# Last two row blocks of w_out in loads over seven, seven and fifteen DMA engines

## Chip, cores and metric

The kernel runs on one core of one Trainium2 chip. The metric is the device time of one execution in microseconds. The kernel before takes 129.38 us (median of three runs, 129.35 to 129.42). The profile comes from one further execution, which took 129.8 us by itself.

## What is computed

One token, a row x of 576 numbers, is normalised (xn) and goes through two branches whose results are added to x.

```python
# A: attention over the last W = 4096 cached keys, 32 query heads, 16 key/value heads, Dh = 128
q = xn @ wq                                   # (576 x 4096)
p = softmax(q . k[-4096:] * Dh**-0.5)
a = (p . v[-4096:]) @ wo                      # (4096 x 576)
# B: gated MLP, F = 4608, Fh = 2304, one position
z = gelu(xn @ w_in)                           # (576 x 4608)
g = w_sp * layernorm(z[Fh:]) + b_sp           # w_sp, b_sp are scalars here
b = (z[:Fh] * g) @ w_out                      # (2304 x 576)
out = x + a + b
```

All inputs are bf16. The caches are 65536 positions long, of which 4096 are read. With the weights that makes 50.96 MB read from HBM, and hardly any arithmetic per byte.

## The kernel before

All large loads are issued by SP, in one order written out by hand (`tc.manual_schedule`): wq (two loads of two 8 KB rows per partition each, L129 and L130), the rest of wq (`wq_h`, L131), w_in (L132 to L134), then the key and value pairs (`load_k`, `load_v` through `load_pair`, L100 to L112), and last, from step u = 13 of the main loop on (L443 to L455), w_out and wo. A pair is a tile of 128 partitions x 16 KB. It comes in one load of 2 MB, or in two halves of 8 KB per partition: the key pairs 0 and 1, and the value pair 7. Six buffers hold pairs, so a load of a pair waits until TensorE is through with the pair six before it.

Every load signals its landing on one of eight semaphores, which are taken in turn. A load therefore also waits until the load eight places before it has landed. In the trace a landing is a row of sixteen increments of the semaphore, one for each DMA engine that carried a share.

TensorE transposes the keys (L338), forms the scores (L355), transposes the probabilities (L372) and multiplies them with the values (L402). At the end it projects: `project` (L457) does two matmuls, one for each half of the 576 outputs: a single column of 128 numbers times 128 x 288 weights, summed into `sps_130` and `sps_131`. I call the two a pair of matmuls. There is a pair for each of 32 columns of the attention output (`wo_sb`) and each of the 18 row blocks of w_out (`wout_sb`).

The row blocks of w_out are grouped by `WOUT_CHUNKS` (L39). An entry (i, t0, t1) is the rows t0 to t1 of each group of nine rows, in half i of w_out; partition p holds rows 9p to 9p+8 of that half. So (0, 0, 9) is one load of 10368 bytes per partition, and (1, 0, 5), (1, 5, 8), (1, 8, 9) are loads of 5760, 3456 and 1152 bytes per partition. In the profile they are `wout_0_310`, `wout_0_311`, `wout_5_312` and `wout_8_313`. The order of the last loads is: value pair 7 in two halves, `wout_0_310`, the five loads of wo, `wout_0_311`, `wout_5_312`, `wout_8_313`. TensorE uses them at the end in the same order, but for `wout_0_310`, which is used before wo (L472, L486). After the last pair of matmuls VectorE and ScalarE each cast one half of the row (L501, L502), and SP stores it (L503).

Of the kernel before, what the change touches and what calls it, by code (L numbers as in the profile page):

```python
# [16 lines left out]
D = 576  # L17
# [14 lines left out]
ZC = 1152  # L32
# [3 lines left out]
NZ1 = 18  # L36
KV_BUFS = 6
WO_CHUNKS = ((0, 0, 8), (1, 0, 8), (2, 0, 8), (3, 0, 4), (3, 4, 8))
WOUT_CHUNKS = ((0, 0, 9), (1, 0, 5), (1, 5, 8), (1, 8, 9))  # L39


@with_exitstack
def kernel(
# [14 lines left out]
    nc = tc.nc  # L58
    P = nc.NUM_PARTITIONS
# [22 lines left out]
    def wrows(src, t0, t1):  # L82
        return src[0:512, :].rearrange("(p t) c -> p t c", t=4)[:, t0:t1, :]

    def whalf(src):
        return src[512:576, :].rearrange("m (c j) -> (m c) j", c=2)

    wq_t = wpool.tile([P, 4, 4096], BF16, name="wq")
# [8 lines left out]
    def pair_rows(cache, jp):  # L97
        return cache[0, 2 * jp:2 * jp + 2, SK - W:SK, :].rearrange("h (k t) d -> k h (t d)", k=64)

    def load_pair(cache, jp, nm, halves):  # L100
        tile_ = kvpool.tile([P, 64, DH], BF16, name=f"{nm}{jp}", tag="kv")
        dst, src = tile_[:].rearrange("p t d -> p (t d)"), pair_rows(cache, jp)
        n = 8192 // halves
        for f in range(halves):
            nc.sync.dma_start(dst[:, n * f:n * (f + 1)], src[:, :, n * f:n * (f + 1)])
        return tile_

    def load_k(jp):
        kn_tiles[jp] = load_pair(A_k_cache, jp, "kn", 2 if jp < 2 else 1)

    def load_v(jp):
        v_tiles[jp] = load_pair(A_v_cache, jp, "v", 2 if jp == 7 else 1)  # L112
# [13 lines left out]
    order = tc.manual_schedule(engines={PE, SP})  # L126
    ctx.enter_context(order)

    for t in range(2):  # L129
        nc.sync.dma_start(wq_t[:, 2 * t:2 * t + 2, :], wrows(A_wq, 2 * t, 2 * t + 2))  # L130
    nc.sync.dma_start(wq_h[:], whalf(A_wq))  # L131
    for t in range(4):  # L132
        nc.sync.dma_start(win_sb[t][:], wrows(B_w_in, t, t + 1).rearrange("p t c -> p (t c)"))
# [143 lines left out]
    def z_columns():  # L277
        zv = zrow[:].rearrange("p (c t) -> p t c", t=9)
        for t in range(9):
            nc.tensor.matmul(  # L280
                fin[:, MZ + 4 * t:MZ + 4 * t + 4], lhsT=zv[:, t, :], rhs=id4f[:], start=True, stop=True,
            )
        zsb = const.tile([P, NZ], FP32, name="zsb")
        nc.vector.tensor_copy(
            zsb[:].rearrange("p (i t) -> p i t", i=4),
            fin[:, MZ:MZ + NZ].rearrange("p (t i) -> p i t", i=4),
        )
        u = const.tile([P, NZ], FP32, name="u_gelu")
        nc.vector.tensor_mul(u[:], zsb[:], zsb[:])
        nc.vector.tensor_scalar(out=u[:], in0=u[:], scalar1=0.044715, scalar2=1.0, op0=ALU.mult, op1=ALU.add)  # L290
        nc.vector.tensor_mul(u[:], u[:], zsb[:])
        th = const.tile([P, NZ], FP32, name="th_gelu")
        nc.scalar.activation(th[:], u[:], ACT.Exp, scale=-2.0 * GELU_C)
        nc.vector.tensor_scalar_add(th[:], th[:], 1.0)
        nc.vector.reciprocal(th[:], th[:])
        G = const.tile([P, NZ], FP32, name="G_gelu")
        nc.vector.tensor_mul(G[:], th[:], zsb[:])
        statz = const.tile([P, 2], FP32, name="statz")
        nc.vector.reduce_sum(statz[:, 0:1], G[:, NZ1:NZ], axis=AXX)
        junk2 = work.tile([P, NZ1], FP32, name="junk")  # L300
        nc.vector.tensor_tensor_reduce(
            out=junk2[:], in0=G[:, NZ1:NZ], in1=G[:, NZ1:NZ], scale=1.0, scalar=0.0,
            op0=ALU.mult, op1=ALU.add, accum_out=statz[:, 1:2],
        )
        return G, statz
# [3 lines left out]
    def z_gate(G, statz):  # L309
        mvz = mean_rstd(statz, FH, "z")  # L310
        z2n = const.tile([P, NZ1], FP32, name="z2n")
        nc.vector.tensor_scalar(out=z2n[:], in0=G[:, NZ1:NZ], scalar1=mvz[:, 0:1], scalar2=mvz[:, 3:4],
                                op0=ALU.subtract, op1=ALU.mult)
        gv = const.tile([P, NZ1], FP32, name="gv")
        nc.vector.tensor_scalar(out=gv[:], in0=z2n[:], scalar1=sb_col[:, 0:1], scalar2=sb_col[:, 1:2],
                                op0=ALU.mult, op1=ALU.add)
        nc.vector.tensor_mul(hv[:], G[:, 0:NZ1], gv[:])

    w2pool = tc.alloc_tile_pool(name="w2pool", bufs=1, reuse_waits="tile")
    wo_sb = [w2pool.tile([P, r1 - r0, D], BF16, name=f"wo{g}_{r0}") for g, r0, r1 in WO_CHUNKS]  # L320
    wout_sb = [w2pool.tile([P, t1 - t0, D], BF16, name=f"wout{i}_{t0}") for i, t0, t1 in WOUT_CHUNKS]

# [8 lines left out]
    def transpose_k(u):  # L331
        jp, half = u // 2, u % 2
        kn = kn_tiles[jp]
        parts = []
        for c in range(4):
            tps = ps_t.tile([P, 8, P], BF16, name=f"ktps{u}_{c}", tag="tps")
            for s in range(8):
                nc.tensor.transpose(tps[:, s, :], kn[:, 32 * half + 8 * c + s, :], ident[:])  # L338
            kT = ktpool.tile([P, 1024], BF16, name=f"kT{u}_{c}", tag="kT")
            src = tps[:].rearrange("p a b -> p (a b)")  # L340
            if c % 2:
                nc.scalar.copy(kT[:], src)
            else:
                nc.vector.tensor_copy(kT[:], src)
            parts.append(kT)
        kT_tiles[u] = parts
# [20 lines left out]
    def transpose_p(g):  # L367
        p_sb = p_tiles.pop(g)
        ptps = ps_t.tile([P, 8, P], BF16, name=f"ptps{g}", tag="tps")
        for b in range(2):  # L370
            for s in range(4):
                nc.tensor.transpose(  # L372
                    ptps[:, 4 * b + s, 0:NR], p_sb[0:NR, b, 128 * s:128 * (s + 1)], ident[0:NR, 0:NR])
        ptq = ptq_sb[g % 2]
        for m in range(2):
            for half in range(2):
                r0 = 8 * half + 4 * m
                for b in range(2):
                    for h in range(2):
                        nc.vector.tensor_scalar(  # L380
                            out=ptq[:, m, half, b, :, :].rearrange("p i (k c) -> p k i c", c=4)[
                                :, 4 * m:4 * m + 4, :, 2 * h:2 * h + 2],
                            in0=ptps[:, 4 * b:4 * b + 4, :].rearrange("p s (i r) -> p s i r", i=4)[
                                :, :, :, r0 + 2 * h:r0 + 2 * h + 2],
                            scalar1=BIG, scalar2=mask2[:, h:h + 1], op0=ALU.min, op1=ALU.mult,
                        )
            nc.vector.tensor_reduce(
                out=psum_all[:, 8 * g + 4 * m:8 * g + 4 * m + 4],
                in_=ptq[:, m, :, :, :, 16 * m:16 * m + 16].rearrange("p f b i (s c) -> p c (f b i) s", c=4),
                op=ALU.add, axis=mybir.AxisListType.XY,  # L390
            )
# [30 lines left out]
    for u in range(22):  # L422
        if u < 16:
            transpose_k(u)
        if u == 0:
            gz = z_columns()
        if u == 1:
            z_gate(*gz)
        if u in (5, 9, 13, 17):
            transpose_p((u - 5) // 4)  # L430
        if u == 17:
            den = ps_t.tile([P, 512], FP32, name="den", tag="tps")
            nc.tensor.matmul(den[0:HQ, 0:1], lhsT=psum_all[:], rhs=ones_f[:, 0:1], start=True, stop=True)
            rden = const.tile([HQ, 1], FP32, name="rden")
            nc.vector.reciprocal(rden[:], den[0:HQ, 0:1])
        if u in (10, 14, 18):
            o_rows((u - 10) // 4)
        if 1 <= u <= 16:
            scores(u - 1)
        if u >= 6:  # L440
            pv(u - 6)
        load_next(more.get(u, 0))
        if u == 13:  # L443
            def load_wout(n):
                i, t0, t1 = WOUT_CHUNKS[n]
                nc.sync.dma_start(
                    wout_sb[n][:],
                    B_w_out[ZC * i:ZC * (i + 1), :].rearrange("(p t) n -> p t n", t=9)[:, t0:t1, :])

            load_wout(0)  # L450
            for n, (g, r0, r1) in enumerate(WO_CHUNKS):
                nc.sync.dma_start(
                    wo_sb[n][:], A_wo[1024 * g:1024 * (g + 1), :].rearrange("(p r) n -> p r n", r=8)[:, r0:r1, :])
            for n in range(1, len(WOUT_CHUNKS)):
                load_wout(n)  # L455
# [8 lines left out]
    def project_b(n, ts):  # L464
        i, t0, t1 = WOUT_CHUNKS[n]
        for t in ts:
# [27 lines left out]
    for n, (g, r0, r1) in enumerate(WO_CHUNKS):  # L494
        for r in range(r0, r1):
            project(oT_all[:, r, g:g + 1], wo_sb[n][:, r - r0, :])
    for n in range(1, len(WOUT_CHUNKS)):
        project_b(n, range(WOUT_CHUNKS[n][1], WOUT_CHUNKS[n][2]))

# [35 lines left out]
```

## Time and profile before

| What | Value |
|---|---|
| median of three runs | 129.38 us |
| the profiled execution | 129.8 us, of which its span 127.8 us |
| read from HBM | 50.96 MB, 399 GB/s over the span |
| DMA queue q1 (all of SP's loads) | 95.3% of sixteen engines' span |
| TensorE busy | 69% of the span, granted clock 0.888 on average |
| DVE and ACT busy | 35% and 33% |
| landing of `wout_0_311` | 122.91 us |
| last matmul starts | 124.76 us |
| store of the output issued | 125.82 us |

The span runs from the first to the last instruction. The profiled execution's own time is 2.0 us longer than its span. "PEclk" is the share of TensorE's full clock that was granted. The "DMA" row is the mean busy share of the sixteen DMA engines.

### The profile page before, as it was taken

To read this page: it belongs to the slowest core of one execution; us is meant where nothing else is said; L and a number is where in the kernel's file an instruction comes from. 1 tells how busy PE (TensorE), PEld (TensorE's weight loads), DVE (VectorE), ACT (ScalarE), POOL (GpSimd) and SP (SyncE) were. 2 spreads that over 40 slices of the span, in tenths; PEclk is the share of its full clock that TensorE was granted. 3 is DMA by queue.
4 is the path that set the end of the run, shared out by engine and by line. 5 is a ranking of instruction groups with operands and counts; after the bars stand their busy time and mean duration, and the time that the engine had idled before them with its cause. 6 is when DMAs were issued, how large, how long until landed. Compare 5 with 4: busy or idle time off the path is not lost.

```text
span 127.8 us, 2524 instructions
## 1 busy us (share of the span) xinstructions
PE 88.5 (69%) x1080; PEld 62.7 (49%) x1080; DVE 45.1 (35%) x161; ACT 41.7 (33%) x50; POOL 3.7 (3%) x10
## 2 busy tenths in 40 slices
PE   1014953463999999895399797299399907977761
PEld 0012221123999688662377475287198404545430
DVE  3043110030307756982033944045842290022001
ACT  4000010010503778655056566049243701031001
POOL 8001000000000100000000000000000000000000
PEclk9999999999995999999657999869959995589975
DMA  5999999999999999999999999999999999999950
GB/s 129 436 421 396 437 430 424 410 422 423 413 446 431 446 410 413 441 421 426 410 436 431 431 426 405 451 415 433 405 441 431 392 428 412 419 430 410 412 205 0
DMA packets 5202, 51.11 MB, mean 400 GB/s; under 512 B 582, under 2 KB 712, under 8 KB 1480
## 3 DMA queue, kind: packets, MB, share of 16 engines
q1 hardware_dynamic: 5186, 50.96, 95.3%
q8 instruction: 8, 0.13, 0.4%
q14 instruction: 2, 0.02, 0.0%
q10 hardware_dynamic: 6, 0.00, 0.0%
HBM read 50.96 MB, written 0.00 MB: 399 GB/s over the span
## 4 chain that ended last, share of the span: by engine, by line
DMA 68%; PE 27%; DVE 2%; SPq 1%; issue 0%; DVEq 0%
DMA kn_816<-in_A_k_cache_dram 18%; DMA kn_101<-in_A_k_cache_dram 17%; DMA wout_0_311<-in_B_w_out_dram 15%; DMA v_1254<-in_A_v_cache_dram 12%; DMA wq<-in_A_wq_dram 6%; PE fin L280 3%; DVE ptq_314 L380 2%; PE sps_130 L355 2%; PE sps_130 L459 2%; PE sps_131 L355 1%; PE ops L402 1%; PE ktps_0_1102 L338 1%; PE ktps_0_318 L338 1%; PE ktps_0_387 L338 1%; PE ktps_2_1124 L338 1%; PE ktps_2_409 L338 1%
## 5 line engine op out<-in xcount | busy, mean ns | idle before, releaser
L338 PEld LDWEIGHTS <-kn_101 128*128 128x128 bf16 x64 | 6.6, 148 | 3.5 <-DMA kn_101<-in_A_k_cache_dram 3.5
L338 PEld LDWEIGHTS <-kn_450 128*128 128x128 bf16 x64 | 5.3, 124 | 4.9 <-DMA kn_450<-in_A_k_cache_dram 4.0
L338 PEld LDWEIGHTS <-kn_816 128*128 128x128 bf16 x64 | 5.1, 123 | 4.0 <-DMA kn_816<-in_A_k_cache_dram 3.6
L338 PEld LDWEIGHTS <-kn_972 128*128 128x128 bf16 x64 | 4.9, 118 | 3.0 <-DMA kn_972<-in_A_k_cache_dram 2.6
L265 PEld LDWEIGHTS <-xz 128*32 128x32 bf16 x60 | 2.3, 123 | 8.3 <-issue 7.0
L237 ACT CAST qrow<-sps_131 128x512 bf16<-128x512 f32 x1 | 0.6, 585 | 12.8 <-PE sps_131 L231 12.8
L338 PEld LDWEIGHTS <-kn_692 128*128 128x128 bf16 x64 | 3.6, 98 | 1.9 <-DMA kn_692<-in_A_k_cache_dram 1.4
L338 PEld LDWEIGHTS <-kn_111 128*128 128x128 bf16 x64 | 3.6, 98 | 1.8 <-DMA kn_111<-in_A_k_cache_dram 0.9
L280 PEld LDWEIGHTS fin<-id4f,zrow 128*128 128x128 f32 x18 | 4.4, 336 | 0.0
L280 PE MATMUL fin<-id4f,zrow 128*128 128x4 f32 x18 | 4.4, 377 | 0.0
L272 ACT COPY zrow<-zps_234 128x384 f32<-128x384 f32 x1 | 0.5, 478 | 11.2 <-PE zps_234 L265 11.2
L271 DVE COPY zrow<-zps_233 128x384 f32<-128x384 f32 x1 | 0.6, 558 | 10.1 <-PE zps_233 L265 10.1
L402 PEld LDWEIGHTS <-ptq_315 128*32 128x32 bf16 x64 | 3.2, 118 | 1.8 <-issue 0.3
L459 PEld LDWEIGHTS <-oT_all 128*1 128x1 bf16 x64 | 2.7, 83 | 2.8 <-issue 1.0
L338 PEld LDWEIGHTS <-kn_107 128*128 128x128 bf16 x64 | 3.6, 98 | 0.9 <-issue 0.9
L338 PEld LDWEIGHTS <-kn_104 128*128 128x128 bf16 x64 | 3.6, 98 | 0.9 <-issue 0.9
L166 PE MATMUL fin<-sb_row,one_row 1*128 1x2 bf16 x1 | 0.2, 182 | 5.3 <-DMA sb_row<-in_B_b_sp_dram 5.3
L231 PE MATMUL sps_130<-wq,xz 128*32 128x512 bf16 x16 | 2.5, 628 | 1.6 <-DVE xz L198 1.6
L502 ACT CAST res<-sps_131 1x288 bf16<-1x288 f32 x1 | 0.4, 389 | 9.8 <-PE sps_131 L459 9.8
L338 PE MATMUL ktps_0_818<-ident,kn_450 128*128 128x128 bf16 x8 | 1.0, 308 | 3.5 <-DMA kn_450<-in_A_k_cache_dram 3.5
L501 DVE CAST res<-sps_130 1x288 bf16<-1x288 f32 x1 | 0.4, 446 | 8.6 <-PE sps_131 L459 8.6
L380 DVE TENSOR_SCALAR ptq_315<-ptps_1409,mask_128 128x32 bf16<-128x32 bf16 x16 | 2.5, 236 | 2.5 <-PE ptps_1409 L372 2.5
(352 smaller groups left out, 233.9 us busy)
## 6 DMA issues: line engine op xcount, KB each, us to landing
wq<-in_A_wq_dram SPq DMA_DIRECT2D x2, 2048.0 KB, 9.5
kn_101<-in_A_k_cache_dram SPq DMA_DIRECT2D x2, 1024.0 KB, 20.2
kn_104<-in_A_k_cache_dram SPq DMA_DIRECT2D x2, 1024.0 KB, 21.3
kn_107<-in_A_k_cache_dram SPq DMA_DIRECT2D x1, 2048.0 KB
v_109<-in_A_v_cache_dram SPq DMA_DIRECT2D x1, 2048.0 KB
kn_111<-in_A_k_cache_dram SPq DMA_DIRECT2D x1, 2048.0 KB, 27.5
v_113<-in_A_v_cache_dram SPq DMA_DIRECT2D x1, 2048.0 KB
kn_450<-in_A_k_cache_dram SPq DMA_DIRECT2D x1, 2048.0 KB
```

The source lines that it names most:

```text
L231: nc.tensor.matmul(sps[b][32 * i:32 * i + 32, :], lhsT=lhsT, rhs=rhs, start=(t == 0), stop=(t == 4), tile_position=(0, 32 * i),)
L237: nc.scalar.copy(qrow[:, 512:1024], sps[1][:])
L265: nc.tensor.matmul(zps[b][32 * i:32 * i + 32, 0:ZB], lhsT=lhsT, rhs=rhs, start=(t == 0), stop=(t == 4), tile_position=(0, 32 * i),)
L271: nc.vector.tensor_copy(zrow[:, 0:ZB], zps[0][:, 0:ZB])
L272: nc.scalar.copy(zrow[:, ZB:2 * ZB], zps[1][:, 0:ZB])
L280: nc.tensor.matmul(fin[:, MZ + 4 * t:MZ + 4 * t + 4], lhsT=zv[:, t, :], rhs=id4f[:], start=True, stop=True,)
L338: nc.tensor.transpose(tps[:, s, :], kn[:, 32 * half + 8 * c + s, :], ident[:])
L355: nc.tensor.matmul(sps[b][32 * i:32 * i + 16, :], lhsT=q_bf[:, g, m, half, :], rhs=parts[c // 2][:, 512 * (c % 2):512 * (c % 2) + 512], st ...
L380: nc.vector.tensor_scalar(out=ptq[:, m, half, b, :, :].rearrange("p i (k c) -> p k i c", c=4)[:, 4 * m:4 * m + 4, :, 2 * h:2 * h + 2], in0 ...
L402: nc.tensor.matmul(ops[32 * i:32 * i + 32, :], lhsT=ptq[:, m, half, b, i, :], rhs=v[:, t0:t0 + 4, :], start=(u % 4 == 0 and b == 0), stop= ...
L459: nc.tensor.matmul(outp[g], lhsT=lhsT, rhs=rhs[:, OC * g:OC * (g + 1)], start=first, stop=last, tile_position=(0, 32 * g),)
L501: nc.vector.tensor_copy(res[:, 0:OC], outp[0])
```

## The change

The last three loads of w_out become five pieces in a different cut. Row block (1, 0, 5) stays. Then come row blocks 5 and 6 in one load over sixteen engines (2304 bytes per partition), and row blocks 7 and 8 in three loads by partitions: 0 to 48, 49 to 97 and 98 to 127, again with 2304 bytes per partition. The two pieces of 49 partitions are carried by seven DMA engines, seven partitions each; the piece of 30 by fifteen, two partitions each. All other large loads are of 128 partitions, eight for each of sixteen engines. Two loads elsewhere are merged: the two loads of wq become one of 32 KB per partition, and key pair 1 comes in one load of 2 MB and no longer in two halves. The number of loads that SP issues stays the same.

```diff
-WOUT_CHUNKS = ((0, 0, 9), (1, 0, 5), (1, 5, 8), (1, 8, 9))
+WOUT_CHUNKS = ((0, 0, 9), (1, 0, 5), (1, 5, 7), (1, 7, 9))
+
+TAIL_ROWS = ((0, 49), (49, 98), (98, 128))
...
-        kn_tiles[jp] = load_pair(A_k_cache, jp, "kn", 2 if jp < 2 else 1)
+        kn_tiles[jp] = load_pair(A_k_cache, jp, "kn", 2 if jp < 1 else 1)
...
-    for t in range(2):
-        nc.sync.dma_start(wq_t[:, 2 * t:2 * t + 2, :], wrows(A_wq, 2 * t, 2 * t + 2))
+    nc.sync.dma_start(wq_t[:], wrows(A_wq, 0, 4))
...
-                nc.sync.dma_start(
-                    wout_sb[n][:],
-                    B_w_out[ZC * i:ZC * (i + 1), :].rearrange("(p t) n -> p t n", t=9)[:, t0:t1, :])
+                dst = wout_sb[n][:].rearrange("p t n -> p (t n)")
+                src = B_w_out[ZC * i:ZC * (i + 1), :].rearrange("(p t) n -> p (t n)", t=9)[:, D * t0:D * t1]
+                for p0, p1 in TAIL_ROWS if n == len(WOUT_CHUNKS) - 1 else ((0, P),):
+                    nc.sync.dma_start(dst[p0:p1, :], src[p0:p1, :])
```

## The prediction

> **What bounds the kernel now.** I read the page first, from its slices and its queues.
>
> ```profile
> DMA  5999999999999999999999999999999999999950
> ...
> q1 hardware_dynamic: 5186, 50.96, 95.3%
> q8 instruction: 8, 0.13, 0.4%
> q14 instruction: 2, 0.02, 0.0%
> ```
>
> The DMA engines are full from the second slice to the 38th, so the stream of 50.96 MB sets the time, and only the head, the tail and the overhead of packets can be won or lost. The ten packets of kind "instruction" are fetches of code: eight of 16 KB, two of 8 KB. Next I read the end of the chain of waits.
>
> ```profile
> 104.31 18.61 DMA wout_0_311<-in_B_w_out_dram
> 122.91 0.04 issue
> 122.96 0.33 PE sps_130 L459
> ...
> 125.31 0.45 DVE res L501
> ```
>
> `wout_0_311` lands at 122.91 us, and TensorE then runs nine pairs of matmuls without a pause; the timeline shows where the two later loads come in.
>
> ```profile
> 123.80 0.45 PE L459 MATMUL sps_130<-wout_0_311,hv 128*1 128x288 bf16 x1
> 124.04 0.45 PE L459 MATMUL sps_130<-wout_5_312,hv 128*1 128x288 bf16 x1
> 124.52 0.45 PE L459 MATMUL sps_130<-wout_5_312,hv 128*1 128x288 bf16 x1
> 124.76 0.45 PE L459 MATMUL sps_130<-wout_8_313,hv 128*1 128x288 bf16 x1
> ```
>
> A pair costs 0.24 us here, because the granted clock fell to 0.50 after 123 us; at full clock earlier pairs start 0.12 us apart. The issues say that `wout_5_312` lands at 106.80 + 17.2 = 124.0 us and `wout_8_313` at 109.96 + 14.3 = 124.3 us. So TensorE's slow run of nine pairs only just covers the last landing: 124.76 - 124.30 = 0.46 us are to spare. Last, the windows of the end, whose final two columns are DMA share and GB/s:
>
> ```profile
> 121.50:122.00 0.50, 0.35 (x6) 0.11 (x3) 0.00 (x0) 0.00 (x0) 0.00 (x0) 1.00 1.08 431
> 122.00:122.20 0.20, 0.00 (x0) 0.00 (x0) 0.00 (x0) 0.00 (x0) 0.00 (x0) 1.00 0.70 271
> 122.80:123.00 0.20, 0.04 (x2) 0.04 (x3) 0.00 (x0) 0.00 (x0) 0.00 (x0) 1.00 0.63 248
> 123.40:123.60 0.20, 0.20 (x6) 0.10 (x4) 0.00 (x0) 0.00 (x0) 0.00 (x0) 0.50 0.46 156
> 123.60:123.80 0.20, 0.20 (x5) 0.10 (x2) 0.00 (x0) 0.00 (x0) 0.00 (x0) 0.50 0.40 144
> 123.80:124.00 0.20, 0.20 (x4) 0.13 (x1) 0.00 (x0) 0.00 (x0) 0.00 (x0) 0.50 0.06 17
> ```
>
> The engines don't end together: about six stop by 122.1, the rest run to 123.9. The sixteen increments of each load's semaphore, which the trace records, say it exactly. For `wout_8_313` six come at 122.51 to 122.90, two at 123.60 and 123.69, eight at 124.03 to 124.30. Those groups match the fetches: eight engines carried 16 KB of code each and are some 1.5 us late, two carried 8 KB and are some 0.9 us late, six carried none. (A 16 KB fetch took 1.02 to 1.12 us in the trace, against 0.61 us for a data packet of that size.) A share moved off the late engines is what could be won, at most 0.8 us, the distance from the mean of the sixteen (123.54) to the last.
>
> **The change, part by part.**
>
> *Merged loads.* Key pair 1: eight packets of 16 KB at 613 ns stand for sixteen of 8 KB at 312 ns on every engine; consecutive packets overlap by 4 ns, so 8 x (2 x 308 - 609) = 0.06 us, and one 9 ns marker packet goes. For wq, a row of 32 KB is not in the trace: at one end it is cut into packets of 16 KB as now (only a marker goes, 0.01 us), at the other it saves as key pair 1 does, 0.06 us more. It can't add packets, so no loss. I take 0.08 us in all: every later landing moves up by that.
>
> What waits for the merged wq: the matmuls on its first half start at 11.40 and would start after the second half's landing, 12.93, so 1.5 us later. The q and first z matmuls end then near 19.4 us; the next w_in load releases matmuls at 19.83 after 1.64 us of waiting, which hides it. Without that cover it would still be hidden, since the DMA stream doesn't wait for these matmuls. Key pair 1 is first transposed at 42.3 us and landed whole at 38.1: hidden. Before the first wait for a landing SP can issue the merged wq, wq_h and w_in's four large loads: 9.2 MB, some 21 us of stream at 430 GB/s. So the shifted turns of the eight semaphores starve nothing.
>
> *Issue at the end.* Each piece waits for the load eight places before it: the first piece takes the place that `wout_8_313` has now (109.96), the second waits for the first load of wo (landed 112.73), the third for the second (115.52). SP has nothing queued behind them but the store, at 125.8. Five issues at 0.33 us each are over by 116 us, while the engines are busy with earlier loads until after 120.5: hidden by 4 us.
>
> *Row blocks 5 to 8.* Now an engine carries 8 packets of 3456 and 8 of 1152 bytes after `wout_0_311`, which step by 131 and 47 ns (135 and 51 ns less the overlap): 1.42 us. A packet of 2304 bytes isn't in the trace; halfway between it steps by 89 ns. Eight engines' worth of equal cut would again be 16 x 89 = 1.42 us. After the change, a piece over seven engines gives each 7 packets, the third piece gives two to fifteen. If both pieces of seven use the same engines, these seven carry 8 + 7 + 7 + 2 = 24 packets, 2.14 us (0.72 more), eight others 10, 0.89 us (0.53 less), the last 8, 0.71 us (0.71 less). If the second piece takes another seven, fourteen carry 17 and nothing moves by more than 0.1 us. I take the same seven: the four packets of ACT's second and third small load, which go over one engine, stand at 5.510, 6.123, 6.736 and 7.349 us, exactly one 16 KB packet (613 ns) apart, so they queue on one and the same engine. No row tells their numbers.
>
> *Which engines are late.* Ten of sixteen are late, so of any seven at least one is. Nine engines get less, ten would need it. If the one among the seven is an 8 KB one, its landing goes from 123.69 to 124.41 us; if it is a 16 KB one, from 124.30 to 125.02. Eight engines of sixteen are of the second kind; if they stand in a row (round the circle), 14 of the 16 placements touch a given seven, and scattered nearly all do. So I take 125.02.
>
> *The end.* The last load now feeds two pairs and not one. With 125.02, pair 17 starts at 125.07 and pair 18, at half clock, at 125.31, against 124.76 now: 0.55 us later. Less 0.08 us: +0.47 us. On the profiled execution that is 129.8 + 0.47 = 130.27; the difference applied to the median gives 129.38 + 0.47 = **129.85 us**. (The profiled execution is 0.4 us over the median; its clock at the end may have been lower than in the other runs. At full clock the last pair starts now at 124.35 and then at 125.19: +0.76 us net.)
>
> [...] The rows show every engine at one speed, 16384 bytes in 609 ns, whether sixteen are busy or seven (135 ns for 3456 bytes at 120.6 and at 123.1). By that, moving rows to idle engines moves time. [...]
>
> **Rivals.**
>
> *Hidden.* Only an 8 KB engine is among the seven. The last landing is 124.41 - 0.08 = 124.33 us, still covered by TensorE's nine slow pairs: pair 17 at 124.52 as now. Then only the merged loads count: 129.30 us, no change. It speaks for it that the chain runs through `wout_0_311`, which isn't touched; against it, the count of eight in sixteen.
>
> *Faster.* The runs without a profile end on the last landing, at full clock, and the late engines stand all among the nine that get less (then the 8 KB fetches must cost less there). The last landing is the late ones' 124.30 - 0.53 = 123.77, one pair more costs 0.12, the merged loads give 0.08: -0.49 us, 128.89 us. It decides from the point where the clock stays at 1.0 past 123 us; that three runs agree within 0.07 us speaks for a landing and not for a clock that falls at some moment.
>
> *Collisions.* The pieces slow each other and the late engines. Priced by the nearest row, a packet beside a fetch, which takes 1.09 us for 0.61: half of the 0.72 us extra again, and twice over the two pieces: at full clock 129.38 + 0.76 + 0.7 = 130.8 us as the far end.
>
> **How the numbers follow.** A measurement tells 0.2% (0.26 us) from no change. Forecast 0.42, collisions 0.08: slower 0.5. Hidden 0.3: same. Faster 0.2. The range takes in faster and hidden, and the forecast up to full clock and a little contention: 128.9 to 130.3 us.
>
> **What would show it.** In the profile after, the last piece's increments: seven engines' shares should land late, one at about 125.0, others about 0.5 us earlier than now; a wait of TensorE on the last load ahead of pair 17; no pause of DMA before 122 us; `wout_0_311` near 122.83. It is wrong if the last landing lies before 124.4 us, if the increments of the two pieces come from fourteen engines, or if the clock at the end differs.

## The result, and the profile after

The changed kernel takes 130.95 us (median of four runs, 130.65 to 131.13) against 129.40 us beside it. The ratio, taken over all executions and not between the medians, is 1.0105, with a 95% interval of 1.0064 to 1.0146: slower by some 1.4 us (0.8 to 1.9), where 0.47 us had been forecast. The profiled execution has a span of 129.1 us, 1.3 us more than before.

The page's DMA slices show the same full stream, but the last slices fall off differently (its GB/s row ends with 410 358 85 0, that of before with 410 412 205 0, in slices that are 1% longer).

```profile
DMA  6979999999999999999999999999999999999930
```

The end of the chain of waits now runs through the last load, where it ran through `wout_0_311` (now named `wout_0_309`):

```profile
115.59 10.20 DMA wout_7_311<-in_B_w_out_dram
125.79 0.14 issue
125.92 0.40 PE sps_128 L461
...
126.67 0.45 DVE res L503
```

The last piece lands at 125.79 us; before, the last landing was at 124.30. In the timeline TensorE pauses before each of the three groups of row blocks:

```profile
123.33 0.28 PE L461 MATMUL sps_128<-wout_0_309,hv 128*1 128x288 bf16 x1 [1.42 <-DMA wout_0_309<-in_B_w_out_dram]
...
124.62 0.28 PE L461 MATMUL sps_128<-wout_5_310,hv 128*1 128x288 bf16 x1 [0.52 <-DMA wout_5_310<-in_B_w_out_dram]
...
125.92 0.40 PE L461 MATMUL sps_128<-wout_7_311,hv 128*1 128x288 bf16 x1 [0.77 <-DMA wout_7_311<-in_B_w_out_dram]
```

The brackets hold the idle time before and what ended it. Even `wout_0_309`, which the change doesn't touch, is used at 123.33 us and not at 122.96. TensorE's slow run of nine pairs, which covered the last landings in the kernel before, is gone: it waits for each load.

Why all three are late is seen in windows of half a microsecond; the last two columns are the DMA share and GB/s. First the kernel before, then the changed one:

```profile
122.00:122.50 0.50, 0.00 (x0) 0.00 (x0) 0.00 (x0) 0.00 (x0) 0.00 (x0) 1.00 0.65 256
...
123.00:123.50 0.50, 0.50 (x6) 0.32 (x7) 0.00 (x0) 0.00 (x0) 0.00 (x0) 0.56 0.55 207
```

```profile
122.00:122.50 0.50, 0.00 (x0) 0.00 (x0) 0.00 (x0) 0.00 (x0) 0.00 (x0) 1.00 0.75 251
122.50:123.00 0.50, 0.00 (x0) 0.00 (x0) 0.00 (x0) 0.00 (x0) 0.00 (x0) 1.00 0.83 249
123.00:123.50 0.50, 0.17 (x4) 0.14 (x5) 0.00 (x0) 0.00 (x0) 0.00 (x0) 1.00 0.69 143
...
124.50:125.00 0.50, 0.38 (x4) 0.09 (x3) 0.00 (x0) 0.00 (x0) 0.00 (x0) 0.77 0.10 37
```

Divide GB/s by share: that is what sixteen engines would move at the speed of those that are busy. Before, at 123.0 to 123.5 us, it is 207 / 0.55 = 376. After, 143 / 0.69 = 207: more engines are busy and together they move less. At 124.5 to 125.0, with only the last few left, it is 370 again. So here busy engines hinder each other while the pieces are under way. The trace's packets say the same: one of 2304 bytes takes 93 ns at best, 117 ns on average and up to 231 ns (the average is over the pieces and the whole load `wout_5_310` together, since the trace doesn't tell them apart).

The semaphore increments of the three pieces, in us (each piece also gets one as SP issues it, left out here):

```
partitions  0 to 48:  122.57 122.64 122.91   124.15   124.45 124.59 124.97
partitions 49 to 97:  123.43 123.63 123.93   124.81   124.94 125.17 125.59
partitions 98 to 127: 122.20 122.33   123.72 123.82 124.12   124.19 124.27 124.28 124.30 124.34 124.35   125.00 125.12 125.37 125.79
```

The first two pieces have three early engines each, one in between and three late: the same seven engines twice, with three of the late ones among them. The third piece fits this: two of its engines finish at 122.20 and 122.33, before any share of the other pieces lands, so they carried neither, and its last four follow the last four of the second piece by 0.18 to 0.20 us. The six from 124.19 to 124.35 must be the late engines outside the seven, with the one in between.

### The profile page after: what moved, and what is told of

Same layout as the page of the kernel before. It is cut to its first block, busy times and chain, and to the rows that moved or that the text cites. A ratio compares the mean times of both kernels' runs of the same rounds, so it can differ in the third digit from the quotient of the medians.

```text
span 129.1 us, 2526 instructions
## 1 busy us (share of the span) xinstructions
PE 86.7 (67%) x1080; PEld 61.7 (48%) x1080; DVE 45.3 (35%) x161; ACT 41.7 (32%) x50; POOL 3.7 (3%) x10
## 4 chain that ended last, share of the span: by engine, by line
DMA 68%; PE 25%; DVE 2%; SPq 2%; issue 1%; DVEq 0%
DMA wo_0_304<-in_A_wo_dram 20%; DMA kn_814<-in_A_k_cache_dram 17%; DMA kn_100<-in_A_k_cache_dram 13%; DMA wq<-in_A_wq_dram 10%; DMA wout_7_311<-in_B_w_out_dram 8%; PE fin L281 3%; PE sps_128 L356 2%; DVE ptq_312 L381 2%; PE sps_129 L356 1%; PE ops L403 1%; SPq L450 1%; PE ktps_0_316 L339 1%; PE ktps_0_385 L339 1%; PE ktps_3_418 L339 1%; PE ktps_2_338 L339 1%; PE ktps_2_407 L339 1%
## 5 line engine op out<-in xcount | busy, mean ns | idle before, releaser
L339 PEld LDWEIGHTS <-kn_100 128*128 128x128 bf16 x64 | 6.9, 152 | 3.4 <-DMA kn_100<-in_A_k_cache_dram 3.4
L339 PEld LDWEIGHTS <-kn_970 128*128 128x128 bf16 x64 | 5.1, 123 | 4.5 <-DMA kn_970<-in_A_k_cache_dram 4.1
L339 PEld LDWEIGHTS <-kn_448 128*128 128x128 bf16 x64 | 4.5, 113 | 3.7 <-DMA kn_448<-in_A_k_cache_dram 3.2
L339 PEld LDWEIGHTS <-kn_690 128*128 128x128 bf16 x64 | 4.2, 109 | 3.1 <-DMA kn_690<-in_A_k_cache_dram 2.6
L339 PEld LDWEIGHTS <-kn_814 128*128 128x128 bf16 x64 | 3.6, 98 | 2.4 <-DMA kn_814<-in_A_k_cache_dram 2.0
L339 PEld LDWEIGHTS <-kn_109 128*128 128x128 bf16 x64 | 3.6, 98 | 1.8 <-DVE ptq_312 L381 1.0
L339 PEld LDWEIGHTS <-kn_103 128*128 128x128 bf16 x64 | 3.6, 98 | 1.2 <-issue 1.2
L339 PEld LDWEIGHTS <-kn_105 128*128 128x128 bf16 x64 | 3.6, 98 | 0.9 <-issue 0.9
L356 PEld LDWEIGHTS <-q_bf 128*16 128x16 bf16 x128 | 2.6, 88 | 2.0 <-issue 0.5
L461 PEld LDWEIGHTS <-hv 128*1 128x1 bf16 x36 | 1.6, 81 | 3.9 <-issue 2.3
```

Of the source, the lines that this page charges most:

```text
L356: nc.tensor.matmul(sps[b][32 * i:32 * i + 16, :], lhsT=q_bf[:, g, m, half, :], rhs=parts[c // 2][:, 512 * (c % 2):512 * (c % 2) + 512], st ...
L461: nc.tensor.matmul(outp[g], lhsT=lhsT, rhs=rhs[:, OC * g:OC * (g + 1)], start=first, stop=last, tile_position=(0, 32 * g),)
```

## The experiments

**Theories.** *Shares*: the unequal shares put 24 packets in place of 16 on late engines. *Collisions*: packets written at the same time into a part of the partitions hinder each other (in the prediction this was a rival). *The rest*: the merged loads, or the other cut of the row blocks, cost something by themselves. In the expectations of the first two runs, "Theory A" stands for the first two of these together, "Rival B" and "Rival C" for the two halves of the third. In that of the loads by themselves, "Theory of ports" stands for collisions that depend on which partitions a load writes, "Theory of engines alone" for a rate that the number of engines sets. Ratios are to the kernel before, in five rounds, with 95% intervals. Where no ratio is given, the kernel ran once, for its trace alone.

**The merges alone.**

```diff
-    for t in range(2):
-        nc.sync.dma_start(wq_t[:, 2 * t:2 * t + 2, :], wrows(A_wq, 2 * t, 2 * t + 2))
+    nc.sync.dma_start(wq_t[:], wrows(A_wq, 0, 4))
...
-        kn_tiles[jp] = load_pair(A_k_cache, jp, "kn", 2 if jp < 2 else 1)
+        kn_tiles[jp] = load_pair(A_k_cache, jp, "kn", 2 if jp < 1 else 1)
```

> The kernel before with only the two merged loads (wq, key pair 1). Theory A (the loss is all in the pieces of the last row blocks): the merges give what the prediction took, 0.06 to 0.16 us less, so a ratio of 0.999 to 1.000. Rival B (part of the loss is in the merges: the head of the stream, the matmuls on wq that wait 1.5 us longer, or other turns of the semaphores): at least 0.4 of the 1.36 us of the whole change, so a ratio of 1.003 or more.

Measured 1.0007 (0.9992 to 1.0022). No loss of the size that the merges would have to cost, and no gain that could be told either.

**The other cut alone.**

```diff
-WOUT_CHUNKS = ((0, 0, 9), (1, 0, 5), (1, 5, 8), (1, 8, 9))
+WOUT_CHUNKS = ((0, 0, 9), (1, 0, 5), (1, 5, 7), (1, 7, 9))
```

> The kernel before with only the other cut of w_out: row blocks 5 and 6, then 7 and 8, each in one load of 128 partitions over sixteen engines; no pieces by partitions, no merges. Theory A (the pieces over seven and fifteen engines cost the time): the last landing stays at about 124.3 us; two pairs of matmuls follow it in place of one, 0 to 0.12 us more, so a ratio of 1.000 to 1.001. Rival C (packets of 2304 bytes or the two pairs behind the last load are what costs): 0.5 us or more, a ratio of 1.004 or more, with packets slower than the 89 to 93 ns that were worked out.

Measured 1.0005 (0.9993 to 1.0018); the last landing is at 124.44 us, and packets of 2304 bytes take 94 ns on average. The window of this kernel that answers to the changed one's 143 GB/s:

```profile
123.00:123.50 0.50, 0.43 (x8) 0.33 (x9) 0.00 (x0) 0.00 (x0) 0.00 (x0) 1.00 0.58 221
```

221 / 0.58 = 381, as in the kernel before. Packet size and two pairs behind the last load cost nothing that shows. *The rest* falls; the loss is in the pieces.

**Equal shares, two pieces.** The cut of the last kernel, and

```diff
+TAIL_ROWS = ((0, 64), (64, 128))
...
+                for p0, p1 in TAIL_ROWS if n == len(WOUT_CHUNKS) - 1 else ((0, P),):
+                    nc.sync.dma_start(dst[p0:p1, :], src[p0:p1, :])
```

> As the kernel with the other cut over sixteen engines, but row blocks 7 and 8 come in two pieces of 64 partitions, each over sixteen engines, four partitions for each. Every engine carries the same number of packets as in the whole load, so only the order in which partitions are written differs. Theory of shares (what counts is how many packets the late engines carry): the same time as with the whole load, a ratio of 1.000 to 1.002. Theory of collisions (packets that sixteen engines write at once into a part of the partitions slow each other): the packets of the pieces take up to twice the 93 ns, eight of them 0.4 to 0.7 us more, so a ratio of 1.003 to 1.006.

Measured 1.0087 (1.0068 to 1.0106), 1.1 us, although every engine carries as many packets as in the whole load. That is more than the theory of collisions had expected (1.003 to 1.006), and shares explain none of it. The window from 122.0, first here, with nearly all engines busy, then with the whole load over sixteen engines:

```profile
122.00:122.50 0.50, 0.05 (x2) 0.00 (x0) 0.00 (x0) 0.00 (x0) 0.00 (x0) 1.00 0.93 224
```

```profile
122.00:122.50 0.50, 0.00 (x0) 0.00 (x0) 0.00 (x0) 0.00 (x0) 0.00 (x0) 1.00 0.78 307
```

224 / 0.93 = 241, against 307 / 0.78 = 394. Packets of 2304 bytes take 113 ns on average here, against 94. The load before the pieces is hit too: it lands at 124.29 us, and at 123.72 with the whole load.

**Equal shares, other partitions.** The same with

```diff
-TAIL_ROWS = ((0, 64), (64, 128))
+TAIL_ROWS = ((32, 96), (0, 32), (96, 128))
```

> As the kernel with two pieces of 64 partitions, all over sixteen engines with equal shares, but the pieces are the partitions 32 to 95, 0 to 31 and 96 to 127. [...] So half of the slow packets go, and about half of the loss of the kernel with two halves (1.0087): ratio 1.003 to 1.006. Rival (any load of fewer than 128 partitions is slow, or more pieces are slower): three pieces lose as much as the two halves or more, 1.008 to 1.013.

Measured 1.0049 (1.0031 to 1.0068): about half of the loss of the two halves, with a piece more; the two intervals just touch. Packets of 2304 bytes take 100 ns on average, against 113 with the two halves and 94 with the whole load. That half of the slow packets would go, as expected, no run had shown before; these means and the ratio are what was measured. So more pieces aren't slower by their number, and it matters which partitions a piece has.

**Loads by themselves.** The kernel's whole work is replaced by

```python
for p0, p1 in ((0, 128), (0, 64), (32, 96), (64, 128), (0, 49), (49, 98), (0, 98)):
    for n in range(8):
        nc.sync.dma_start(buf[p0:p1, n, :], src[n % 2][p0:p1, :])
    nc.vector.memset(buf[:, :, 0:2], 0.0)
```

> Loads by themselves: this kernel leaves out the whole computation and stores x. It loads rows of w_out, 10368 bytes per partition, eight loads at a time, into the partitions 0 to 127, then 0 to 63, 32 to 95, 64 to 127, 0 to 48, 49 to 97 and 0 to 97; a write of VectorE to the tile parts the stages. Theory of ports: 400 to 430 GB/s for the 128 partitions and for 32 to 95, half of it (200 to 220) for 0 to 63 and 64 to 127; less than seven and fourteen engines' 185 and 370 GB/s for the runs of 49 and 98. Theory of engines alone: 400 to 430 GB/s for all three pieces of 64, 185 for 49 and 370 for 98.

The page's GB/s row, 40 slices of 4.7 us, and the writes of VectorE that end the second to the sixth stage (the bracket is the stage's length, the wait for its first and last bytes included):

```profile
GB/s 184 425 425 431 434 367 164 206 204 206 212 142 201 389 423 146 219 201 206 212 208 73 146 161 146 150 139 104 58 186 195 186 186 111 314 303 294 310 299 168
```

```profile
56.71 0.07 DVE L72 MEMSET buf<- 128x8 uint32 x1 [28.27 <-DMA buf<-in_B_w_out_dram]
73.27 0.07 DVE L72 MEMSET buf<- 128x8 uint32 x1 [16.49 <-DMA buf<-in_B_w_out_dram]
101.75 0.07 DVE L72 MEMSET buf<- 128x8 uint32 x1 [28.42 <-DMA buf<-in_B_w_out_dram]
133.08 0.07 DVE L72 MEMSET buf<- 128x8 uint32 x1 [31.26 <-DMA buf<-in_B_w_out_dram]
157.19 0.07 DVE L72 MEMSET buf<- 128x8 uint32 x1 [24.05 <-DMA buf<-in_B_w_out_dram]
```

Within the stages the row reads: all partitions 425 to 434 GB/s; 0 to 63, some 206; 32 to 95, 389 and 423; 64 to 127, some 206; 0 to 48, some 146; 49 to 97, some 187; 0 to 97, some 303. The same number of bytes and partitions, over as many engines, takes 28.3 us on partitions 0 to 63 and 16.5 us on 32 to 95. The engines aren't idle in the slow stages: the windows inside the first and the second stage have the same DMA share (next to last) at half the GB/s.

```profile
1.00:26.00 25.00, 0.00 (x0) 0.00 (x0) 1.00 0.96 399
29.00:56.00 27.00, 0.00 (x0) 0.00 (x0) 1.00 0.95 197
```

These are the collisions by themselves: sixteen engines that write only the lower 64 partitions, or only the upper 64, get half the rate (some 206 GB/s against 425 to 434 for all 128). (The rows that are read move with the partitions; but all three stages of 64 partitions read unbroken blocks of 0.66 MB from the same two halves of w_out, so the reading side hardly explains that one of them is fast.) Seven engines on 0 to 48 get 146 GB/s where seven get 187 on 49 to 97, which lie on both sides of 64. What makes the partitions differ is not shown: the run gives the rates and not their cause.

**Nearly equal shares, the change's runs of seven.** The cut over sixteen engines with the loop over `TAIL_ROWS`, as for the two halves, and

```diff
+TAIL_ROWS = ((0, 98), (98, 128))
```

> The cut of the change without the merges, but row blocks 7 and 8 in two pieces, of 98 partitions (fourteen engines, seven partitions each) and of 30 (fifteen engines, two each). Fourteen engines carry 17 packets after wout_0_311, one 10, one 8; in the changed kernel seven carry 24. Theory of shares alone: one packet more than 16 on the late engines, 0.09 us, ratio 1.000 to 1.002. Theory of collisions alone: the partitions are written in the same runs of seven as in the change, so at least half of its loss stays, ratio 1.004 to 1.010. If both count, the difference to the changed kernel (1.0105) is what the seven engines' 24 packets add, 0.2 to 0.5%.

Measured 1.0076 (1.0059 to 1.0094). Shares alone would give 1.002 at most by the expectation.

**The pieces without the merges.** The same with

```diff
-TAIL_ROWS = ((0, 98), (98, 128))
+TAIL_ROWS = ((0, 49), (49, 98), (98, 128))
```

> The change without the merged loads: pieces of 49, 49 and 30 partitions. Against the kernel with pieces of 98 and 30 (1.0076), the same partitions are written in the same runs of seven, but seven engines carry 24 packets and not 17. If the unequal shares cost nothing beside the collisions: 1.007 to 1.008. If the seven packets more on a late engine count beside the collisions: up to 0.6 us more, 1.009 to 1.013. Either way the merges are not in it, so it should stand at the changed kernel's 1.0105 within its interval.

Measured 1.0125 (1.0103 to 1.0148), an interval that doesn't overlap with that of the kernel just before. The difference of the two is 0.0049 x 129.4 = 0.63 us, and seven packets at 89 ns make 0.62 us. The two intervals leave some 0.4 us to either side, so that the hundredths agree is luck. The profiled executions say 0.5: the last landing is at 125.70 us here and at 125.19 there, while the load before the pieces lands at 124.43 and 124.42. So shares count too, beside the collisions. That the seven packets alone make the difference is argued: three pieces also write the partitions in another order than two.

**Which engines are late.** Ahead of the unchanged `wout_0_311`, seven extra loads:

```diff
+            probe = w2pool.tile([P, 8, 64], BF16, name="probe")
+            for n, k in enumerate((2, 4, 6, 8, 10, 12, 14)):
+                nc.sync.dma_start(probe[0:k, n, :], A_wq[0:k, 0:64])
```

> The kernel before with seven small extra loads (2, 4, 6, 8, 10, 12 and 14 rows of 128 bytes, read for nothing) between the last load of wo and wout_0_311; each goes over as many engines as it has rows. The landing increments of each load show which engines are late. Theory of shares: among the first six or eight engines there are at least one that is 1.5 us late and one that is 0.8 us late, and the engines beyond the fourteenth are not the latest. Rival (the seven engines are all early, and the loss comes from collisions alone): the increments of the loads of 2, 4 and 6 rows all come early, within 0.4 us of each other. The time itself says little, since the last loads of w_out are issued later here: some 1 to 2 us more.

Increments of the first four, in us:

```
2 engines:  119.51                        120.44
4 engines:  119.69 119.70                 120.58 120.62
6 engines:  119.80 119.87 119.88          120.77 120.80   121.18
8 engines:  119.79 119.99 120.05 120.06   120.95 120.97   121.34 121.38
```

Of the first two engines one is early and one in between; of the first six three are early, two in between and one late. So the first engines are no early ones, and the first half of the shares theory's expectation holds. (The second half can't be told: the load over fourteen engines was issued only at 120.4 us.) But it isn't the same set as in the changed kernel, whose first seven hold one in between and three late: which engines are late differs from run to run or kernel to kernel. The issues of w_out's last loads were late here, and the time (132.36 us) is not used.

**Why they are late.** The kernel before, leaving out half of the key transposes:

```diff
-        for c in range(4):
+        for c in range(2):
...
-        kT_tiles[u] = parts
+        kT_tiles[u] = parts + parts
```

> The kernel before, leaving out half of the key transposes (each score uses the first two of four transposed parts twice), which is 512 instructions of TensorE fewer out of 2160. Theory of code fetches (each 16 KB fetch makes one DMA engine about 1.5 us late for the rest of the run): two fetches fewer, so the last loads show six increments at the latest time and not eight, and eight early ones in place of six. Rival (the engines are late for another reason): again eight late, two in between, six early. The time itself tells nothing of it.

The queues of this run's page, where the kernel before had eight large fetches and two small ones:

```profile
q8 instruction: 6, 0.10, 0.3%
q14 instruction: 1, 0.01, 0.0%
```

Six fetches of 16 KB and one of 8 KB thus come before the last loads. The last load's increments: nine from 122.57 to 123.00 us, one at 123.57, six from 124.15 to 124.47. Six late, one in between, nine early: each fetch makes one engine late, 16 KB by 1.5 us. (Nine and not eight, since there was one small fetch fewer too.)

The 1.5 us are more than a fetch takes (1.02 to 1.12 us) by what the next packet loses. In the trace of before, a packet of 16 or 8 KB starts as the fetch ends behind seven of the eight large fetches, and takes 0.45 to 0.55 us more than usual; at 46.37 us, for instance, one of 16 KB takes 1.09 us in place of 0.61.

## Why the prediction failed

The direction and the mechanism that it took for the likeliest were there; the size was a third of what came. A second mechanism, priced as an unlikely rival and put at nothing in the sum, acted as well and cost about as much as the first.

- *Merged loads, 0.08 us less.* Not to be told from nothing (1.0007, interval 0.9992 to 1.0022). What waits for wq was hidden, as was said.
- *Issue at the end.* Right: the three pieces are issued from 110.03 to 115.9 us, as worked out, and the engines have earlier loads until after 121.
- *The same seven engines carry both pieces.* Right, by the increments.
- *A late engine is among the seven.* Right; there are three.
- *Row blocks 5 to 8: 24 packets at 89 ns.* This is the step that failed. The count was right, and what more packets on a late engine cost was near (0.5 to 0.63 us between the two kernels that differ by seven packets, 0.62 worked out). But the step of 89 ns, from rows of loads that write all 128 partitions, was carried over to loads that write a part of them. With the whole load over sixteen engines the packets take 94 ns on average, 4 ns of it overlap by the prediction's reading; here they take 117 ns, and they slow others: `wout_0_309` lands at 123.28 us where 122.83 was forecast. The last landing was forecast at 125.02 - 0.08 = 124.94 and came at 125.79, 0.85 us later. Nor did the engines that carry less gain by it: the late ones outside the seven were to end 0.53 us earlier, by 123.7, and end at 124.19 to 124.35.
- *The end.* Pair 17 starts at 125.92 and pair 18 at 126.11, against 125.07 and 125.31 with 0.08 us less, so the end is late by hardly more than the landing. TensorE's clock was 1.0 until 124.8 us here and half after it; the two last pairs start 0.19 us apart, where the forecast had 0.24.
- *Collisions left out of the sum.* They stood as a rival with a chance of 0.08, and the sum had nothing for them. The row that spoke for moving rows to idle engines, packets as fast with seven engines busy as with sixteen, couldn't tell, since in the trace of before every large load writes all 128 partitions. The price of 0.7 us was near by luck: it takes half as much again, where its row (1.09 us for 0.61) says 0.8 as much again. The pieces of 98 and 30 lose 0.0076 x 129.4 = 0.98 us, of which one packet more is 0.09, so 0.9 us for collisions. With this the sum would be 0.9 + 8 x 0.089 = 1.6 us, what the pieces alone lose (0.0125 x 129.4 = 1.6); but it is worked out afterwards from that very run and the one beside it, so it tests nothing. The changed kernel's 1.0105 lies 0.0020 lower, but within intervals.
- *Hidden, faster.* Both would have needed another placement of the late engines. With the collisions probably neither was open: the two halves lose 1.1 us with equal shares. No run has such a placement, so this is argued.
- *Small slips.* The mean of the sixteen increments is 123.56 us and not 123.54, and the loads ahead of SP's first wait are 9.4 MB and not 9.2. Neither changes the sum.

Left open: whether moving a late engine's rows to an early one would win anything without collisions. No kernel here gives engines unequal shares without them. Why the packet behind a fetch is slow isn't shown either.

## What to carry to other kernels

A load of fewer than 128 partitions can cost more than its bytes, as the two halves of 64 did here (1.1 us lost on 0.29 MB): before cutting one by partitions, ask which partitions are written at the same moment, and not only how many engines carry it. A second mechanism that can act together with the first belongs into the sum with a price; it isn't an alternative to the one that is already there. To find such hindrance in a profile, divide GB/s by the DMA share: here it fell from some 380 to 207 while engines were busy with packets no smaller.

## What was not expected of the hardware

- Two halves of 64 partitions lose 1.1 us on a load of only 128 x 2304 bytes = 0.29 MB, which takes some 0.7 us at the stream's 430 GB/s. The load ahead of it, still under way on the late engines, lands 0.57 us later as well.
- The same 5.3 MB, loaded by themselves, take 28.3 us into partitions 0 to 63 and 16.5 us into 32 to 95.
- Each 16 KB fetch of code leaves one DMA engine 1.5 us behind for the rest of the run, so that the last load over all engines has its early shares landed from 122.51 us and its last at 124.30. With eight large and two small fetches eight engines were late and two in between; with six large and one small, six and one.
